# Loading the first queries of an attention kernel as two halves on two DMA queues

## The chip, the cores and the metric

The kernel runs on one core of a Trainium2 chip. The metric is the device time of one execution in microseconds (us); less is better. The core has five engines with their own instruction streams: PE (TensorE, matmuls and transposes), DVE (VectorE), ACT (ScalarE, which also issues DMAs), POOL (GpSimd, which issues most of the loads) and SP (SyncE, which only issues DMAs). They wait for each other through semaphores.

## The reference

The kernel computes an attention layer with a sigmoid in place of the softmax, and feeds it to a two-layer network. In short:

```
q, k, v: 8 batches x 12 heads x 448 positions x 64, float32
scores = q @ k.T / 8 - log(448)
attn   = sigmoid(scores) @ v                 # per batch and head
x      = attn, heads side by side            # 3584 x 768
h      = x @ w_in                            # 768 x 2048
out    = (h * sigmoid(h)) @ w_out            # 2048 x 768, float32
```

## The kernel before

**Groups, units, chunks.** The attention is cut into 24 groups `g` of four heads (one batch and one third of its heads). A group's q, k and v are each a tile of 128 partitions x 2 x 7 x 64: the partition holds 64 blocks of positions for two heads, the index `i` of size 2 (called j in later lines) tells the two pairs of heads apart, and the seven chunks `c` are 7 x 64 columns. A unit is one chunk of k against all of q: four matmuls of 64x64 weights into the PSUM tile `psc`, and one sigmoid on ACT (`scores`, L252 to L266) that writes `attnT`. `values` (L274) multiplies `attnT` by v. The later stages, h and the output product, are given out in small steps between the units, in an order written out by hand (`behind`, L734 to L757, then the loops from L788 on).

**How q and k get transposed.** Scores need q and k with the head dimension on the partitions. `pe_transpose` (L193) multiplies pieces of them by an identity on PE, two matmuls per chunk, into a one-bank PSUM tile (`ptrq`, `ptrk`), and copies that to `qT` or `kT`, on DVE (L208) unless the piece names `act_copy` (L191).

**The start.** All other groups are loaded by POOL, whose DMAs also convert to float16 (`load`, L120). The first group's q, and the first two chunks of its k, take another way, through `load_first` (L131): they are loaded as float32 into a scratch tile `qs` by SP and ACT, and then cast to float16 by DVE and ACT. With `FIRST, SPLIT = 2, 4` these are q's chunks 0 to 3 (256 KB, on SP), k's chunks 0 and 1 (128 KB, on ACT) and q's chunks 4 to 6 (192 KB, on ACT behind k). `load_first` is a generator that issues the loads and yields (destination, source) pairs for the casts, `casts[0]` to `casts[3]`: q's chunks 0 and 1, q's chunks 2 and 3 (both on DVE, L663 and L664), k's first chunks and q's rest (both on ACT, by `act_copy`, L665 and L666). The rest of k's first group (160 KB) comes through POOL.

**The order on each engine at the start.** PE begins with `keep_busy(30, P)` (L712, L188), thirty matmuls of 128 columns on a dummy tile. Then come (L713 to L717) the transposes of q's chunks 0 and 1, of q's 2 and 3, of k's 0 and 1 (copied by ACT), of q's 4 to 6; then `scores_of_part(0, SPLIT)`, which multiplies k's first two chunks with q's first four into one two-bank tile (eight matmuls, L237) and applies one sigmoid of 1024 columns (L244); then the transposes of k's chunks 2 and 3 and 4 to 6; then `scores_of_part(SPLIT, NCH)` with q's last three chunks and a sigmoid of 768 columns. From there on each unit has a sigmoid of 896 columns (L266). There are two `psc` tiles at this stage, so PE can be two units ahead of ACT. `after_transpose(0)` (L671) gives POOL the loads of group 3.

The few lines that set the order:

```
    nc.vector.tensor_copy(*casts[0])
    nc.vector.tensor_copy(*casts[1])
    act_copy(*casts[2])
    act_copy(*casts[3])
...
    keep_busy(30, P)
    pe_transpose(0, (("q", 0, 2), ("q", 2, SPLIT), ("k", 0, FIRST, act_copy)))
    pe_transpose(0, (("q", SPLIT, NCH),))
    scores_of_part(0, SPLIT)
    pe_transpose(0, (("k", FIRST, 4), ("k", 4, NCH)))
    scores_of_part(SPLIT, NCH)
```

Of the kernel before, what the change touches and what calls it, by code (L numbers as in the profile page):

```python
# [12 lines left out]
AF = mybir.ActivationFunctionType  # L13
# [4 lines left out]
def kernel(  # L18
# [9 lines left out]
    nc = tc.nc  # L28

    B, H, S, D = q.shape  # L30
    NT, DMODEL = out.shape
    DFF = moe_w_in.shape[1]
    P = 128
    HP = P // 2
    NCH = S // HP
# [10 lines left out]
    QKSCALE = 1.0 / math.sqrt(D)  # L46
# [42 lines left out]
    def one_bank(name):  # L89
        if "any" in banks:  # L90
            ring.append(ring.pop(0))
            return banks["any"].tile([P, 512], F32, tag=f"any{ring[-1]}", name=name)
        taken["single"] += 1
        return banks["single"].tile([P, 512], F32, tag="single", name=name)

    def two_banks(name):
        taken["double"] += 1
        return banks["double"].tile([P, 2, 512], F32, tag="double", name=name)
# [10 lines left out]
    flat = {}  # L109
# [4 lines left out]
    def rows_in(name, g):  # L114
        b, iq = divmod(g, NQ)
        return source[name][b, 4 * iq : 4 * iq + 4].rearrange(
            "(i h) (p c) d -> (h p) i (c d)", h=2, c=NCH
        )
# [10 lines left out]
    FIRST, SPLIT = 2, 4  # L129

    def load_first():  # L131
        room = cpool.tile([P, NHC * NO2 // 2], F32, tag="T2", name="qs")
        at = 0
        for name, c0, c1, eng in (
            ("q", 0, SPLIT, nc.sync),
            ("k", 0, FIRST, nc.scalar),
            ("q", SPLIT, NCH, nc.scalar),
        ):
            size = 2 * (c1 - c0) * D
            st = room[:, at : at + size]  # L140
            at += size
            eng.dma_start(
                st.rearrange("p (i e) -> p i e", i=2), rows_in(name, 0)[:, :, c0 * D : c1 * D]
            )
            st = st.rearrange("p (i c d) -> p i c d", i=2, d=D)
            step = 2 if c0 == 0 else NCH - SPLIT
            for c in range(c0, c1, step):
                yield flat[name, 0][:, :, c : c + step], st[:, :, c - c0 : c - c0 + step]

    ident = cpool.tile([P, P], F16, tag="ident", name="ident")  # L150
    bias_s = cpool.tile([P, 1], F32, tag="biass", name="bias_s")
# [26 lines left out]
    def new_qkT(g):  # L178
        for name in ("k", "q"):
            qkT[name, g] = p3.tile([P, NCH, P], F16, tag=f"{name}T", name=f"{name}T")  # L180
# [4 lines left out]
    def keep_busy(n, cols=512):  # L185
        pw = one_bank("pw")
        for _ in range(n):
            nc.tensor.matmul(pw[:, :cols], dummy[:, :P], dummy[:, :cols], start=True, stop=True)  # L188

    def act_copy(o, i):  # L190
        nc.scalar.activation(o, i, AF.Copy)  # L191

    def pe_transpose(g, pieces=(("k", 0, 4), ("k", 4, NCH), ("q", 0, 4), ("q", 4, NCH))):  # L193
        if ("k", g) not in qkT:
            new_qkT(g)
        for name, c0, c1, *copy in pieces:
            dst = qkT[name, g].rearrange("p c t -> p (c t)")
            ptr = one_bank(f"ptr{name}")
            for c in range(c0, c1):
                for j in range(2):  # L200
                    nc.tensor.matmul(
                        ptr[j * D : (j + 1) * D, (c - c0) * P : (c - c0 + 1) * P],
                        flat[name, g][:, j, c, :],
                        ident,
                        start=True,
                        stop=True,
                    )
            (copy[0] if copy else nc.vector.tensor_copy)(  # L208
                dst[:, c0 * P : c1 * P], ptr[:, : (c1 - c0) * P]
            )  # L210
# [12 lines left out]
    first_attnT = cpool.tile([P, NQ * DFF // 2], F16, tag="SI1", name="attnT")  # L223
    first_attnT = first_attnT[:, : FIRST * 2 * S].rearrange("p (c j s) -> p c j s", c=FIRST, j=2)
# [3 lines left out]
    def scores_of_part(c0, c1):  # L228

        size = (c1 - c0) * HP  # L230
        psc = two_banks("psc")
        for ch in range(FIRST):
            for half in range(2):
                own = slice(half * HP, (half + 1) * HP)
                for j in range(2):
                    rows = slice(j * D, (j + 1) * D)
                    nc.tensor.matmul(  # L237
                        psc[own, j, ch * size : (ch + 1) * size],
                        qkT["k", 0][rows, ch, own],
                        qkT["q", 0][rows, c0:c1, own],  # L240
                        start=True,
                        stop=True,
                    )
        nc.scalar.activation(  # L244
            first_attnT[:, :, :, c0 * HP : c1 * HP],
            psc[:, :, : FIRST * size].rearrange("p j (c s) -> p c j s", c=FIRST),
            AF.Sigmoid,
            bias=bias_s,
            scale=QKSCALE,
        )  # L250

    def scores(g, ch):  # L252
        attnT[g, ch] = p12.tile([P, 2, S], F16, tag="attnT", name="attnT")
# [395 lines left out]
    new_flat("q", 0)  # L649
    new_flat("k", 0)  # L650
    casts = list(load_first())
    load("k", 0, FIRST, NCH)
    make_identity(nc, ident)
# [7 lines left out]
    nc.vector.memset(dummy[:, P:], 0.5)  # L661
    nc.scalar.activation(warm, bias_s, AF.Sigmoid, bias=bias_s, scale=1.0)
    nc.vector.tensor_copy(*casts[0])  # L663
    nc.vector.tensor_copy(*casts[1])  # L664
    act_copy(*casts[2])  # L665
    act_copy(*casts[3])  # L666

    units = [(g, ch) for g in range(NQB) for ch in range(NCH)]
# [40 lines left out]
            return True  # L709
        return False  # L710

    keep_busy(30, P)  # L712
    pe_transpose(0, (("q", 0, 2), ("q", 2, SPLIT), ("k", 0, FIRST, act_copy)))  # L713
    pe_transpose(0, (("q", SPLIT, NCH),))
    scores_of_part(0, SPLIT)
    pe_transpose(0, (("k", FIRST, 4), ("k", 4, NCH)))
    scores_of_part(SPLIT, NCH)  # L717
    after_transpose(0)

# [152 lines left out]
```

## Time and profile before

| | before |
|---|---|
| median of 3 runs (lowest to highest) | 364.97 us (364.74 to 366.23) |
| the profiled execution | 365.24 us |
| its span, first to last instruction | 363.2 us |
| around the span | 2.0 us |
| busy: PE / DVE / ACT / POOL | 355.9 / 252.7 / 249.4 / 76.8 us |

The span is the stretch that the trace shows; all times below count from its start. "Busy" is the time in which an engine had an instruction of its own at work; PE's matmuls overlap, so its 98% says that matmuls nearly always were under way, not that PE ran at its peak. A line of the timeline gives start, duration, engine, source line, operation, the tile written and those read, the shape, how many equal instructions were put together, and in brackets how long the engine stood idle before it and for whom.

### The profile page before, as it was taken

What the parts mean: (1) busy time and instruction counts of PE and PEld (TensorE: products, weight loads), DVE (VectorE), ACT (ScalarE), POOL (GpSimd) and SP (SyncE); (2) the same over time, 40 slices, a digit from 0 to 9 for tenths busy, and PEclk for the clock granted to TensorE, in tenths of its full rate; (3) what the DMA queues carried; (4) which work ended last, traced back from release to release, by engine and by line L of the source; (5) the groups of instructions that cost most, each with busy time, mean ns of one, the idle gap of its engine ahead of it and who ended that gap; (6) DMA issues with size and microseconds to landing.
All of it is one profiled execution on the core that took longest, in us unless ns stands there. A gap on an engine that the chain in (4) does not pass through costs nothing. (4 is left out here: it accounts for less than half of the span.)

```text
span 363.2 us, 7654 instructions
## 1 busy us (share of the span) xinstructions
PE 355.9 (98%) x3038; PEld 186.3 (51%) x3038; DVE 252.7 (70%) x461; ACT 249.4 (69%) x339; POOL 76.8 (21%) x115
## 2 busy tenths in 40 slices
PE   8999999999999999999999999999999999999995
PEld 5554445555555555555555455554555555556662
DVE  3665469777666587868566768795856677797763
ACT  5999886489989756688777756679899956640000
POOL 7566521040060272000033047000100000000000
PEclk9999999999999999999999999999999999999999
DMA  8999999979979599008679569902883120003333
GB/s 156 199 204 204 204 205 203 172 116 174 170 109 216 117 138 167 0 2 163 105 132 197 100 139 152 127 2 51 160 107 88 24 65 0 3 0 88 87 88 87
DMA packets 65859, 42.87 MB, mean 118 GB/s; under 512 B 35872, under 2 KB 62496, under 8 KB 65824
## 3 DMA queue, kind: packets, MB, share of 16 engines
q0 software_dynamic: 26800, 22.52, 42.2%
q1 hardware_dynamic: 38320, 19.34, 27.4%
q8 instruction: 24, 0.39, 0.5%
q10 hardware_dynamic: 704, 0.52, 0.4%
q14 instruction: 11, 0.09, 0.1%
HBM read 45.61 MB, written 11.01 MB: 156 GB/s over the span
## 5 line engine op out<-in xcount | busy, mean ns | idle before, releaser
L266 ACT ACTIVATE attnT<-psc,bias_s 128x896 f16<-128x896 f32 x166 | 156.1, 1009 | 20.0 <-PE psc L259 18.7
L538 PEld LDWEIGHTS <-S 128*128 128x128 f16 x448 | 42.0, 98 | 33.6 <-issue 8.1
L259 PE MATMUL psc<-qT,kT 64*64 64x448 f16 x664 | 48.3, 360 | 1.1 <-ACT attnT L244 0.5
L301 DVE TENSOR_SCALAR xT<-pav 128x448 f16<-128x448 f32 x48 | 27.7, 620 | 29.1 <-PE pav L290 29.1
L124 POOL DMA_DIRECT2D vf<-in_v_dram x24 | 17.3, 722 | 131.3 <-PE pav L290 116.8
L538 PEld LDWEIGHTS <-gTr 128*128 128x128 f16 x336 | 31.0, 98 | 27.3 <-issue 8.7
L538 PE MATMUL po<-w_out_sb,gTr 128*128 128x384 f16 x224 | 41.6, 327 | 0.0
L412 PEld LDWEIGHTS <-w_in_sb 128*128 128x128 f16 x288 | 27.9, 98 | 26.7 <-issue 1.1
L538 PE MATMUL po<-T,S 128*128 128x384 f16 x224 | 41.0, 327 | 0.0
L538 PE MATMUL po<-w_out_sb,S 128*128 128x384 f16 x224 | 40.8, 326 | 0.0
L322 PE MATMUL ph<-xT,w_in_sb 128*128 128x448 f16 x192 | 38.5, 353 | 0.0
L290 PE MATMUL pav<-attnT,vf 64*64 64x448 f16 x672 | 38.1, 351 | 0.1
L412 PE MATMUL pa<-xT,w_in_sb 128*128 128x448 f16 x144 | 33.2, 353 | 0.0
L259 PEld LDWEIGHTS <-kT 64*64 64x64 f16 x664 | 17.6, 104 | 27.8 <-issue 21.6
L412 PEld LDWEIGHTS <-SI 128*128 128x128 f16 x216 | 21.1, 98 | 20.0 <-issue 0.5
L290 PEld LDWEIGHTS <-vf 64*64 64x64 f16 x672 | 21.6, 106 | 12.4 <-issue 2.9
L322 PEld LDWEIGHTS <-w_in_sb 128*128 128x128 f16 x192 | 17.8, 98 | 18.9 <-issue 3.4
L428 ACT ACTIVATE part<-pa 128x448 f32<-128x448 f32 x24 | 12.8, 542 | 18.0 <-PE pa L412 18.0
L538 PE MATMUL po<-T,gTr 128*128 128x384 f16 x112 | 21.9, 327 | 0.6 <-DVE osb L559 0.6
L406 ACT ACTIVATE gTr<-pc 128x448 f16<-128x448 f32 x24 | 13.1, 544 | 12.9 <-DVE pc L422 12.5
L422 DVE TENSOR_TENSOR part<-pb,part 128x448 f32<-128x448 f32 x24 | 14.9, 622 | 8.3 <-ACT part L428 5.0
L191 ACT ACTIVATE m<-po 128x384 f32<-128x384 f32 x1 | 0.5, 491 | 27.3 <-PE po L538 27.3
(80 smaller groups left out, 473.0 us busy)
## 6 DMA issues: line engine op xcount, KB each, us to landing
out_dram<-osb SPq DMA_DIRECT2D x52, 192.0 KB, 3.2
vf<-in_v_dram POOLq DMA_DIRECT2D x24, 224.0 KB, 7.2
kf<-in_k_dram POOLq DMA_DIRECT2D x23, 224.0 KB, 6.8
qf<-in_q_dram POOLq DMA_DIRECT2D x23, 224.0 KB, 7.5
w_in_sb<-in_moe_w_in_dram POOLq DMA_DIRECT2D x16, 192.0 KB, 7.9
w_out_sb<-in_moe_w_out_dram POOLq DMA_DIRECT2D x4, 768.0 KB, 14.9
out_dram<-osb SPq DMA_DIRECT2D x6, 96.0 KB, 2.2
kT<-kr SPq DMA_TRANSPOSE x18, 4.5
```

Of the source, the lines that this page charges most:

```text
L124: nc.gpsimd.dma_start(flat[name, g][:, :, c0:c1].rearrange("p i c d -> p i (c d)"), rows_in(name, g)[:, :, c0 * D : c1 * D],)
L191: nc.scalar.activation(o, i, AF.Copy)
L259: nc.tensor.matmul(psc[own, j, :S], qkT["k", g][rows, ch, own], qkT["q", g][rows, :, own], start=True, stop=True,)
L266: nc.scalar.activation(attnT[g, ch], psc[:, :, :S], AF.Sigmoid, bias=bias_s, scale=QKSCALE)
L290: nc.tensor.matmul(pav[half][j * D : (j + 1) * D, :S], flat["v", g][own, j, ch, :], at[own, j, :], start=(ch == 0), stop=(ch == NCH - 1),)
L301: nc.vector.tensor_scalar_mul(xT[b][:, half * NQ + iq, :], pav[half][:, :S], SX)
L322: nc.tensor.matmul(ph[:, :S], w_in_sb[:, cc, fc * P : (fc + 1) * P], xT[b][:, cc, :], start=(at == 0), stop=(at == NCC - 1),)
L406: nc.scalar.activation(gTr[:, r * NG + i, col + c * S : col + (c + 1) * S], h, AF.Silu, bias=0.0, scale=ISX)
L412: nc.tensor.matmul(to, w[:, n, i * P : (i + 1) * P], x[:, n], start=(start and n == 0), skip_group_check=not start, stop=(n == NQ - 1),)
L422: nc.vector.tensor_add(o, po, x)
L428: nc.scalar.activation(got[i, 1], bank[i, "a"], AF.Copy)
L538: nc.tensor.matmul(po[:, :NO2], a[:, fc, :], w[:, fc, :], start=(fc == 0), stop=(fc == NHC - 1))
```

## The change

The first loads are cut differently. q's chunks 0 to 3 become two loads of 128 KB, the half `i` = 0 on SP and the half `i` = 1 on ACT; behind each stands one half of k's first two chunks (64 KB each); q's chunks 4 to 6 stand third on SP. The casts follow the halves: DVE casts the first half of q and of k, ACT the second half of both, and q's rest is cast on DVE, behind the two copies to `qT` in DVE's order. On PE the transposes of q's chunks 4 to 6 move behind the first scores, and there are 26 dummy matmuls instead of 30. In the first `scores_of_part` the sigmoid of 1024 columns becomes two of 512, one for each chunk of k.

```
     def load_first():
         room = cpool.tile([P, NHC * NO2 // 2], F32, tag="T2", name="qs")
+        both = slice(0, 2)
         at = 0
-        for name, c0, c1, eng in (
-            ("q", 0, SPLIT, nc.sync),
-            ("k", 0, FIRST, nc.scalar),
-            ("q", SPLIT, NCH, nc.scalar),
+        for name, c0, c1, parts in (
+            ("q", 0, SPLIT, ((nc.sync, slice(0, 1)), (nc.scalar, slice(1, 2)))),
+            ("k", 0, FIRST, ((nc.sync, slice(0, 1)), (nc.scalar, slice(1, 2)))),
+            ("q", SPLIT, NCH, ((nc.sync, both),)),
         ):
-            size = 2 * (c1 - c0) * D
-            st = room[:, at : at + size]
-            at += size
-            eng.dma_start(
-                st.rearrange("p (i e) -> p i e", i=2), rows_in(name, 0)[:, :, c0 * D : c1 * D]
-            )
-            st = st.rearrange("p (i c d) -> p i c d", i=2, d=D)
-            step = 2 if c0 == 0 else NCH - SPLIT
-            for c in range(c0, c1, step):
-                yield flat[name, 0][:, :, c : c + step], st[:, :, c - c0 : c - c0 + step]
+            size = (c1 - c0) * D
+            st = room[:, at : at + 2 * size].rearrange("p (i e) -> p i e", i=2)
+            at += 2 * size
+            for eng, i in parts:
+                eng.dma_start(st[:, i], rows_in(name, 0)[:, i, c0 * D : c1 * D])
+                yield (
+                    flat[name, 0][:, i, c0:c1],
+                    st[:, i].rearrange("p i (c d) -> p i c d", d=D),
+                )
...
-        nc.scalar.activation(
-            first_attnT[:, :, :, c0 * HP : c1 * HP],
-            psc[:, :, : FIRST * size].rearrange("p j (c s) -> p c j s", c=FIRST),
-            AF.Sigmoid,
-            bias=bias_s,
-            scale=QKSCALE,
-        )
+        step = 1 if c0 == 0 else FIRST
+        for ch in range(0, FIRST, step):
+            nc.scalar.activation(
+                first_attnT[:, ch : ch + step, :, c0 * HP : c1 * HP],
+                psc[:, :, ch * size : (ch + step) * size].rearrange(
+                    "p j (c s) -> p c j s", c=step
+                ),
+                AF.Sigmoid,
+                bias=bias_s,
+                scale=QKSCALE,
+            )
...
     nc.vector.tensor_copy(*casts[0])
-    nc.vector.tensor_copy(*casts[1])
-    act_copy(*casts[2])
+    act_copy(*casts[1])
+    nc.vector.tensor_copy(*casts[2])
     act_copy(*casts[3])
...
-    keep_busy(30, P)
+    keep_busy(26, P)
     pe_transpose(0, (("q", 0, 2), ("q", 2, SPLIT), ("k", 0, FIRST, act_copy)))
-    pe_transpose(0, (("q", SPLIT, NCH),))
+    nc.vector.tensor_copy(*casts[4])
     scores_of_part(0, SPLIT)
-    pe_transpose(0, (("k", FIRST, 4), ("k", 4, NCH)))
+    pe_transpose(0, (("q", SPLIT, NCH), ("k", FIRST, 4), ("k", 4, NCH)))
     scores_of_part(SPLIT, NCH)
```

## The prediction, made before the changed kernel was run

> **What bounds the kernel now.** I first read the busy times by stage, since the shares over the whole span mix stages. The columns are the stretch, its length, and the busy time (instructions) of PE, PE's weight loads, DVE, ACT, POOL, then clock, DMA share and rate.
>
> ```profile
> 4.20:8.50 4.30, 3.62 (x53) 1.84 (x50) 2.86 (x7) 3.08 (x5) 3.58 (x6) 1.00 1.19 167
> 8.50:28.60 20.10, 19.67 (x300) 10.50 (x299) 12.15 (x22) 19.99 (x24) 12.45 (x20) 1.00 1.24 200
> 28.60:54.40 25.80, 25.56 (x263) 11.63 (x260) 14.35 (x26) 23.08 (x33) 12.34 (x17) 1.00 1.29 204
> 54.40:204.60 150.20, 149.69 (x1279) 76.95 (x1276) 110.36 (x204) 113.40 (x147) 32.57 (x48) 1.00 0.85 138
> ```
>
> From 8.5 to 28.6 ACT is busy 19.99 of 20.10 us. From 28.6 on ACT has gaps and waits for PE, whose idle time there, by the list of waits, is a few tenths of a us in all. So the kernel has three parts: a start that ends with the first sigmoid, an ACT stream to 28.6, and then PE to the end. The change touches only the start; what it wins or loses is how much sooner or later ACT's stream flows without a break. ACT's timeline shows where that is.
>
> ```profile
> 4.46 0.42 ACT L191 ACTIVATE kf<-qs 128x256 f16<-128x256 f32 x1 [1.06 <-DMA qs<-in_k_dram]
> 4.99 0.52 ACT L191 ACTIVATE qf<-qs 128x384 f16<-128x384 f32 x1
> 5.61 0.38 ACT L191 ACTIVATE kT<-ptrk 128x256 f16<-128x256 f32 x1
> 6.75 1.91 ACT L244 ACTIVATE attnT<-psc,bias_s 128x1024 f16<-128x1024 f32 x2 [0.75 <-PE psc L237]
> 8.54 20.16 ACT L266 ACTIVATE attnT<-psc,bias_s 128x896 f16<-128x896 f32 x22
> ```
>
> The stream starts at 6.75 and doesn't stop: the second sigmoid lasts 0.89 (the groups by form), so it started at 6.75 + 1.91 - 0.89 = 7.77; the third at 8.54. Then I followed the start back on the other engines.
>
> ```profile
> 4.24 0.29 DVE L663 CAST qf<-qs 128x256 f16<-128x256 f32 x1 [2.82 <-DMA qs<-in_q_dram]
> 4.45 0.43 DVE L664 CAST qf<-qs 128x256 f16<-128x256 f32 x1
> ...
> 4.59 0.77 PE L201 MATMUL ptrq<-ident,qf 128*64 128x128 f16 x8
> ...
> 5.05 0.77 DVE L208 CAST qT<-ptrq 128x256 f16<-128x256 f32 x2 [0.17 <-PE ptrq L201]
> 5.15 0.43 PE L201 MATMUL ptrk<-ident,kf 128*64 128x128 f16 x4
> ...
> 6.05 0.64 PE L237 MATMUL psc<-qT,kT 64*64 64x256 f16 x8
> ```
>
> The chain is: q lands at 4.24, DVE casts 0.29, PE transposes from 4.59; k's transposes stand behind them from 5.15; ACT copies kT 5.61 to 6.00; first scores 6.05; sigmoid 6.75, 0.70 later.
>
> **When the halves land.** Today SP's load of q, issued at 0.74, lands 3.5 later; ACT's load of k, issued at the same time, 3.7 later. This is from the DMA view of 2.4 to 3.2 (packets, MB, share of 16 engines; q1 is SP's queue, q10 ACT's):
>
> ```profile
> q1 hardware_dynamic: 156, 0.15, 59.6%
> q10 hardware_dynamic: 134, 0.07, 28.2%
> ```
>
> Before 2.4, q1 had sent 75 packets and q10 none: q's second half is under way together with k. With the change the packets of k come behind q on both queues. How much sooner a half of 128 packets lands, the trace bounds from two sides. Late end: as now, 4.24. Early end: at 356.95 SP and ACT each issue a store of 64 rows and 96 KB at the same moment:
>
> ```profile
> out_dram<-osb SPq DMA_DIRECT2D x1, 96.0 KB, 2.1
> out_dram<-osb ACTq DMA_DIRECT2D x1, 96.0 KB, 2.4
> ```
>
> If the halves went like these, SP's would land at 0.74 + 2.1 = 2.9 and ACT's at 3.15. A half has 128 rows, between 64 and q's 256 today. Straight between 2.4 us at 64 and 3.7 at 256 lies 2.8; the start of the kernel is busier than its end, so I take 3.05, a little above: ACT's half lands at 3.8, SP's before it. ACT is free then (its table load and warm activation end at 3.40).
>
> [...]
>
> **The change part by part.**
> - *Casts of q.* ACT needs 0.42 for 128x256 where DVE needs 0.29. The first transposes can start at 3.8 + 0.02 + 0.42 + 0.05 (the delay from cast to PE today: 4.59 - 4.53) = 4.29, against 4.59. All eight then run without the second wait that splits them today, so k's begin 0.43 later (four pairs at 0.107, the pace of the dummies: (3.38 - 0.31)/29) instead of 0.56: 4.72.
> - *k.* Its ACT half stands behind q's half, both on the queue and on ACT. Bounds on its landing: no earlier than q's half (3.8), no later than ACT's second load today (4.96, issued at 1.27). Two stores in a row on SP land 0.62 apart (issued at 358.25 and 358.77); so 3.8 + 0.6 = 4.4. Cast of 128x128 about 0.30 (0.42 at 256, 0.29 for one column), 0.06 to PE: 4.76, as good as PE's 4.72. Then, as today, 0.46 to kT's copy, 0.39 for it, 0.05 to PE: scores at 5.65 against 6.05, the first sigmoid at 6.35 against 6.75.
> - *q's rest.* Third on SP, issued at about 1.78 (each issue blocks 0.5) instead of 1.27. With today's 3.7 it lands at 5.47 instead of 4.96. DVE reaches its cast behind the two qT copies (4.29 + 1.16 = 5.45), so the load is just hidden. Cast of 384 columns about 0.45 (0.29 to 0.43 at 256): 5.92. PE has issued the scores by then; transposes from 6.0, copy from 6.45 (0.46 later) to 7.0 (0.56), second scores 7.05, its sigmoid 0.43 later at about 7.47. The first sigmoids leave ACT free at 6.35 + 1.02 = 7.37. **So q's rest is late next**, by 0.1: of 0.40 won, 7.77 - 7.47 = 0.30 remains. k's rest moves behind three more pairs on PE; its copies end near 7.9, as today (6.97 + 0.89), so POOL's load of group 3, which waits for them, isn't moved by more than 0.2.
> - *Two sigmoids for one.* In the built order the first of the two holds the wait for all eight score matmuls and the second none, so the first doesn't start sooner. Cost: sigmoids of 448 columns follow at 0.43 (two in 0.98, one lasts 0.55), those of 896 at 0.92 (20.16/22); two small ones cost no more than a big one. Bounds -0.05 to +0.2 (if the table's 0.3 for one column were paid bare); I take 0.
> - *Dummies.* 26 end their issue at 1.06 + 26 x 0.107 = 3.84, before 4.29; thirty would end at 4.27. Cost 0. SP has nothing else until its transposes at 61 us; POOL's order is unchanged.
> - *Does the gain reach the end?* Loads must be there 0.3 sooner. The closest: group 3's q, issued at 8.35, takes 8.8, lands at 17.14, used at 18.13; w_in's first quarter lands at 24.41, used at 25.43. Slack 1.0 covers 0.3 and POOL's 0.2. Without that cover, the gain stops there.
>
> **Sum.** -0.30 on the profiled 365.24 (363.2 span and 2.0 around it): 364.94. That execution is 0.27 above the median of the runs, so against 364.97 it is 364.67, 364.7.
>
> **Rivals.**
> 1. *The halves land no sooner*, because the engines, and not the order of the queues, set q's end. ACT's half at 4.24 gives transposes at 4.24 + 0.02 + 0.47 = 4.73, scores at 6.06, q's rest cast from 5.89, its sigmoid near 7.9: +0.1, **365.1**. For it: from 2.8 to 4.5 the engines are nearly always busy. Against: k's 134 packets no longer compete in that stretch. [...]
> 2. *Slower: five loads start one after the other.* First packets today come near 1.9, 2.5 and 3.2 (in the trace's packets the loads are told apart by size, 1024, 512 and 768 bytes), for three loads of which two were issued together. If every load costs such a step of 0.65, whatever its size, k's second half starts at 3.8 and q's rest at 4.45, landing 1.7 later (as 3.25 to 4.96) at 6.15. From landing to sigmoid it is 2.0 by the terms above, so it decides from a landing at 5.75; at 6.15 the sigmoid comes at 8.15, +0.4: **365.4**. Against it: the 0.3 between the small stores at 356.95.
> 3. *PE's clock stays low longer.* Pairs of transposes go at 0.107 until 5.8, but ten (five pairs) take 0.47 at 6.62: PE got faster there. If a gap of PE ahead of the first transposes (0.45 instead of 0.35) put that off by several us, a unit with its two dummies would take about 1.5 instead of ACT's 0.92 for four units: +2.2, **367.2**. It needs a gap that matters; the one before 4.59 didn't.
> 4. *The split does start early*, after four of the eight matmuls (0.22 sooner): only if the wait isn't as I read it, and q's rest still holds the next: **364.5**.
>
> **How the numbers follow.** Forecast 52%, own range 364.4 to 365.0 (best: halves at 3.5 and q's rest hidden, -0.5). Rival 1: 22%. Rival 2: 18%. Rival 3: 4%. Rival 4: 4%. The range runs from 364.4 less 0.3 (the three runs' median lies 0.23 above their lowest) to rival 2's late end (landing at 6.4, +0.65) and 0.3: 364.1 to 365.9. 0.5%, about what a measurement can tell from no change, is 1.8 us; only rival 3 is beyond it. Faster 0.02, same 0.94, slower 0.04.
>
> **What would show it.** ACT's cast of q starts near 3.8; first scores near 5.65; the first of two sigmoids near 6.35, the 768-column one near 7.47 with a short wait for PE; the 22 sigmoids start near 8.25 instead of 8.54, and the span is 0.3 shorter. A cast at 4.2 or later speaks for rival 1; an ACT wait of 0.4 or more ahead of the 768-column sigmoid for rival 2; a break in ACT's stream or a wait of PE for a load between 10 and 30 us would make the forecast wrong.

## The result, and the profile after

The changed kernel takes 367.5 us (median of 6 runs, 366.59 to 368.07) against 365.0 (6 runs, 364.64 to 366.23): ratio 1.0064, 95% interval 1.0044 to 1.0083. It is slower by 0.64%, where 364.7 and a range up to 365.9 were forecast. The profiled execution took 367.21 us with a span of 365.2, 2.0 more than the 363.2 of before; all of it is lost ahead of 31 us.

By stage (columns as in the prediction's first view), the loss stands in the start and in ACT's stream:

```profile
4.20:8.50 4.30, 2.14 (x44) 1.47 (x43) 1.93 (x6) 1.93 (x5) 2.71 (x5) 1.00 1.19 196
8.50:28.60 20.10, 19.53 (x296) 9.70 (x292) 11.56 (x22) 18.99 (x21) 13.16 (x20) 0.92 1.25 201
```

PE is busy for 2.14 us between 4.2 and 8.5 instead of 3.62, and between 8.5 and 28.6 its mean clock is 0.92 instead of 1.00. ACT's timeline says the same from the other side:

```profile
3.81 0.42 ACT L192 ACTIVATE qf<-qs 128x256 f16<-128x256 f32 x1 [0.55 <-DMA qs<-in_q_dram]
...
6.07 1.27 ACT L247 ACTIVATE attnT<-psc,bias_s 128x512 f16<-128x512 f32 x2 [0.52 <-PE psc L238]
8.77 0.90 ACT L247 ACTIVATE attnT<-psc,bias_s 128x768 f16<-128x768 f32 x1 [1.43 <-PE psc L238]
9.57 1.00 ACT L271 ACTIVATE attnT<-psc,bias_s 128x896 f16<-128x896 f32 x1
10.78 1.01 ACT L271 ACTIVATE attnT<-psc,bias_s 128x896 f16<-128x896 f32 x1 [0.21 <-PE psc L264]
12.19 2.81 ACT L271 ACTIVATE attnT<-psc,bias_s 128x896 f16<-128x896 f32 x3 [0.40 <-PE psc L264]
15.22 15.61 ACT L271 ACTIVATE attnT<-psc,bias_s 128x896 f16<-128x896 f32 x17 [0.23 <-PE psc L264]
```

The cast of q's half starts at 3.81 and the first sigmoid at 6.07, sooner than before (6.75) as forecast. Then ACT stands idle for 1.43 us. The first of the 22 sigmoids of 896 columns starts at 9.57 instead of 8.54, 1.03 late. And the 22 no longer follow each other: they end at 15.22 + 15.61 = 30.83, after 21.26 us instead of 20.16. So 1.03 us is lost before the stream and 1.10 within it.

What ACT waited for, on DVE and PE:

```profile
6.89 0.36 DVE L719 CAST qf<-qs 128x384 f16<-128x384 f32 x1 [1.40 <-DMA qs<-in_q_dram]
```
```profile
5.60 0.41 PE L238 MATMUL psc<-qT,kT 64*64 64x256 f16 x8 [0.47 <-ACT kT L192]
7.31 0.36 PE L202 MATMUL ptrq<-ident,qf 128*64 128x128 f16 x6 [1.29 <-DVE qf L719]
...
9.18 1.03 PE L189 MATMUL pw<-dummy 128*128 128x512 f16 x2
```

DVE waits for the load of q's chunks 4 to 6, and PE for DVE: from the end of the first scores at 6.0 it has nothing to do until 7.31. After that its two dummy matmuls of 512 columns take 1.03 together, where they took 0.60 in the kernel before:

```profile
8.23 0.60 PE L188 MATMUL pw<-dummy 128*128 128x512 f16 x2
```

The DMA view of the first 2 us shows the late load (KB, us to landing; the last line is from the kernel before):

```profile
qs<-in_q_dram SPq DMA_DIRECT2D x1, 192.0 KB, 5.2
kf<-in_k_dram POOLq DMA_DIRECT2D x1, 160.0 KB, 5.5
qs<-in_q_dram SPq DMA_DIRECT2D x1, 128.0 KB, 2.8
qs<-in_q_dram ACTq DMA_DIRECT2D x1, 128.0 KB, 3.0
```
```profile
qs<-in_q_dram ACTq DMA_DIRECT2D x1, 192.0 KB, 3.7
```

q's rest took 5.2 us, issued at 1.66 and landed at 6.87; in the kernel before 3.7. The halves took 2.8 and 3.0. The load did not start late: its packets (768 bytes, told apart by size) begin 2.0 us after its issue in both kernels. In the kernel before they run from 3.25 to 4.49, which is 1.24 us; in the changed one from 3.70 to 6.51, which is 2.81. And this is PE's clock, in two stretches that follow each other (columns as above; the third number from the end is the clock):

```profile
5.09:8.50 3.41, 1.27 (x33) 0.86 (x32) 1.56 (x5) 1.65 (x3) 1.82 (x4) 1.00 1.23 200
8.50:11.91 3.41, 3.41 (x24) 0.67 (x16) 0.56 (x2) 2.81 (x3) 2.13 (x3) 0.50 1.24 196
```

The trace's clock records put the fall to 0.50 at 8.50 and the return at 11.91. In the 3.41 us before the fall PE was busy for 1.27.

The theory to be tested: **two causes, one behind the other.** q's rest lands late, which costs 1.0; and PE's idle time while waiting for it makes the clock fall for the next 3.41 us, which costs 1.1 more. Rivals: the moved cast and transposes cost by themselves; the load is late because it is third on its queue; the clock has nothing to do with the gap.

### The profile page after: what moved, and what is told of

It is laid out like the page before. It is cut to its first block, busy times and chain, and to the rows that moved or that the text cites. A ratio compares the mean times of both kernels' runs of the same rounds, so it can differ in the third digit from the quotient of the medians.

```text
span 365.2 us, 7652 instructions
## 1 busy us (share of the span) xinstructions
PE 356.4 (98%) x3034; PEld 185.9 (51%) x3034; DVE 252.8 (69%) x462; ACT 249.6 (68%) x340; POOL 76.7 (21%) x115
## 5 line engine op out<-in xcount | busy, mean ns | idle before, releaser
L427 DVE TENSOR_TENSOR part<-pc,part 128x448 f32<-128x448 f32 x24 | 15.0, 624 | 6.1 <-PE pc L417 5.5
```

Of the source, the lines that this page charges most:

```text
L427: nc.vector.tensor_add(o, po, x)
```

## The experiments

Each was timed beside the kernel before on the same chip. There are four groups, and in them the kernel before took 364.84 us (18 runs; e1 to e4), 364.74 (23 runs; e5 to e8), 364.86 (17 runs; e9 and e10) and 364.71 (15 runs; e11).

### e1_busy_gap: PE kept busy while it waits

```
     scores_of_part(0, SPLIT)
+    keep_busy(5)
     pe_transpose(0, (("q", SPLIT, NCH), ("k", FIRST, 4), ("k", 4, NCH)))
```

> The changed kernel with five dummy matmuls of 512 columns put between the first scores and the transposes of q's chunks 4 to 6, where PE stood idle for 1.29 us. Theory: of the 2.1 us by which ACT's stream ends later (30.83 against 28.70), 1.0 comes from the late landing of q's rest and 1.1 from PE running at half clock from 8.5 to 11.9, because it had been idle for most of the 3.4 us before. Then the dummies keep the clock at 1.0, the sigmoids of 896 columns follow without a wait for PE, and the time is about 366.4, 1.1 less than the changed kernel's 367.5; q's rest lands as late as before (6.9). Rival: the half clock has nothing to do with this gap (its phase, or the four dummies fewer at the start): the clock falls all the same, 367.5 or more.

Measured: 366.06 us (365.92 to 366.47), ratio 1.0036 (1.0024 to 1.0048). In its profile the first line is PE's busy time in the stretch behind the rise of the clock (5.21), the second ACT's stream:

```profile
5.21:8.62 3.41, 2.49 (x37) 1.27 (x37) 1.47 (x5) 1.56 (x3) 1.80 (x4) 1.00 1.21 196
```
```profile
9.57 20.12 ACT L271 ACTIVATE attnT<-psc,bias_s 128x896 f16<-128x896 f32 x22
```

The stream starts at 9.57, exactly as late as in the changed kernel, since q's rest lands at 6.91; but the 22 sigmoids run without a break in 20.12. The clock stayed at 1.00. Dummy work that computes nothing brings 1.3 us: the changed kernel lost 2.5 against the kernel before of its own group, this one 1.2 against its own (by the two ratios it is 1.0). What is left, 1.2 us, is the late load.

### e2_pool_held and e6_all_pool_held: POOL's loads out of the way

```
     make_identity(nc, ident)
+    nc.gpsimd.tensor_copy(gate, casts[4][1][:1, 0, 0, :1])
     load("kq", 1)
```

The copy to `gate` makes POOL wait for q's rest. In e6 it stands ahead of `load("k", 0, FIRST, NCH)` too.

> The changed kernel, in which POOL's loads of group 1 and later wait until q's rest has landed (only k's rest of the first group stays ahead). Theory: q's rest, third on SP, starts its packets at 3.7 and shares the 16 engines with POOL's loads, and so takes 5.2 instead of 3.7 us; without them, but still beside k's rest, it lands at about 6.0 or sooner, and the second sigmoid comes at about 7.9 instead of 8.77: 365.2 to 366.5. Rival: it is late because it starts late, as third on its queue: it lands at 6.7 as before and the time is 367.5, or more, since the other loads are now late too (group 1's k would land near 9.3 and is used near 10).

> The changed kernel, in which every load of POOL, k's rest of the first group too, waits until q's rest has landed; the total gets worse (k's rest is late by some 4 us) and only the landing of q's rest is asked. Theory: third on SP it is late because POOL's slow packets take turns with its own: alone it lands at 5.6 or sooner (first packet at 3.7, 1.3 for the 256 packets as in the kernel before, 0.45 to the landing). Rival: it is late because a third load on a queue starts and runs late: 6.3 or later, as in e2_pool_held (6.51).

Measured: in e2 q's rest took 4.9 us and landed at 6.51, in e6 3.3 us, landing at 4.97. In e6 its cast on DVE doesn't wait for it any more:

```profile
4.41 0.76 DVE L209 CAST qT<-ptrq 128x256 f16<-128x256 f32 x2 [0.18 <-PE ptrq L202]
5.08 0.35 DVE L720 CAST qf<-qs 128x384 f16<-128x384 f32 x1
```

So the place on the queue isn't the cause: third on SP and issued at 1.69, the load is as quick as ever when it is alone (3.3). Its place matters only in that POOL's packets begin first. The cause is that it shares the engines with POOL's loads, and above all with the one beside it: of the 1.90 us between 4.97 and 6.87, k's rest (160 KB, landing at 6.34 in e2) makes up 1.54, the loads behind it 0.36. These shares come from one profile each, and the landing of an unchanged load differs by up to 0.5 between profiles (q's 256 KB landed at 4.22 in the kernel before and at 3.74 in e8), so the 0.36 is not shown to be more than chance. The first of e2's two theories had the right cause and the wrong share.

In the kernel before, q's rest ran beside POOL's load too, but had a head start: its packets began at 3.25 and POOL's at 3.78. Here are the queues while q's rest is under way, first in the kernel before from 3.8 to 4.5 (q10 carries q's rest and the last of k, q0 is POOL's), then in the changed kernel from 3.7 to 6.51 (q1 carries q's rest; POOL's packets began at 3.42):

```profile
q0 software_dynamic: 152, 0.10, 93.5%
q10 hardware_dynamic: 127, 0.09, 37.0%
```
```profile
q0 software_dynamic: 431, 0.31, 78.4%
q1 hardware_dynamic: 272, 0.20, 31.1%
```

Before, 146 of the load's 256 packets of data began ahead of POOL's first; in the changed kernel none did, and all ran beside POOL's. With POOL held, in e6, they took 1.34 us (3.28 to 4.62), much like the 1.24 of before.

The times of e2 and e6, 367.78 us (ratio 1.0081, 1.0068 to 1.0094) and 367.82 (a single run), show the other side: held loads are missed later, which e2's first theory (365.2 to 366.5) had left out. In e6 PE waits for k's rest:

```profile
PE ptrk L202 <- DMA kf<-in_k_dram: 2.3, 1, 2.3
```

(us in total, times, longest.) In both the clock fell too, from 7.82 to 11.23 and from 9.16 to 12.57, 3.41 us each.

### e3_rest_second: q's rest ahead of POOL's traffic

```
-            ("k", 0, FIRST, ((nc.sync, slice(0, 1)), (nc.scalar, slice(1, 2)))),
+            ("k", 0, FIRST, ((nc.scalar, both),)),
             ("q", SPLIT, NCH, ((nc.sync, both),)),
```

The casts follow the new order of the loads.

> The changed kernel with q's chunks 4 to 6 as second load on SP, directly behind q's first half, and the first two chunks of k as one load of 128 KB, second on ACT. Theory (the place of q's rest on its queue, ahead of POOL's traffic, decides): it is issued at 1.21 and lands near 5.0, k near 4.4; first sigmoid at 6.3, the 768-column one directly behind it near 7.4; PE has no gap over 0.5 us and keeps its clock: 364.5 to 365.0. Rival (the split of the loads itself costs, or the moved transposes and cast do): slower than 365.5.

Measured: 365.94 us (364.88 to 366.25), ratio 1.0025 (1.0013 to 1.0036). The landing came out as the theory said, 4.68 for q's rest and 4.41 for k; the time, above 365.5 in five of six runs, did not. The profile shows a late clock: it rose only at 10.34, and so the first eight scores took 0.64 us and ten transposes of k 0.75, where e1 has 0.41 and 0.45, and ACT waited for PE twice.

```profile
8.10 0.90 ACT L247 ACTIVATE attnT<-psc,bias_s 128x768 f16<-128x768 f32 x1 [0.38 <-PE psc L238]
8.90 4.95 ACT L271 ACTIVATE attnT<-psc,bias_s 128x896 f16<-128x896 f32 x5
14.09 15.60 ACT L271 ACTIVATE attnT<-psc,bias_s 128x896 f16<-128x896 f32 x17 [0.24 <-PE psc L264]
```

### e4_order_only and e5_order_filled: the moved transposes alone

In e4 the loads are those of before; only the cast of q's rest and its transposes are moved. e5 adds one line:

```
     pe_transpose(0, (("q", 0, 2), ("q", 2, SPLIT), ("k", 0, FIRST, act_copy)))
-    pe_transpose(0, (("q", SPLIT, NCH),))
+    nc.vector.tensor_copy(*casts[3])
+    keep_busy(4, P)                      # e5 only
     scores_of_part(0, SPLIT)
-    pe_transpose(0, (("k", FIRST, 4), ("k", 4, NCH)))
+    pe_transpose(0, (("q", SPLIT, NCH), ("k", FIRST, 4), ("k", 4, NCH)))
```

> The kernel before, with its loads and thirty dummies, of which only the cast of q's chunks 4 to 6 goes from ACT to DVE, behind the two qT copies, and their transposes behind the first scores, as in the changed kernel. Theory: this move costs nothing by itself, since this load lands at 4.96; the first scores come some 0.1 sooner and the second sigmoid stays within 0.3 of 7.77: 364.7 to 365.4. Rival: the move is what costs (the copies queue up behind one another on DVE, PE's gap grows and its clock falls): 366 or more.

> The kernel before with only the moved cast and transposes of q's chunks 4 to 6 (as in e4_order_only), and four dummy matmuls of 128 columns put between k's first transposes and the first scores, where the moved transposes had stood. [...] With the slot filled the full clock comes in the first 7 us in every run again: 364.6 to 364.9, and a spread of the runs under 0.7 (e4_order_only: 364.55 to 366.15). Rival: e4_order_only's loss is the later second part itself (its copies queue up on DVE): then the dummies bring nothing, 365.4 with the same spread.

Measured: e4 365.38 us, ratio 1.0015 (1.0005 to 1.0026), but its twelve runs fall into two heaps: six from 364.55 to 364.88, six from 365.89 to 366.15. Neither theory had foreseen that. e5: 364.76 (364.46 to 365.02, 11 runs), ratio 0.9999 (0.999 to 1.0008); the upper heap is gone. e4's profile is of the upper heap, and its clock rose at 10.27. Where the clock falls and comes back, its records stand 3.41 us apart (8.50 and 11.91 in the changed kernel); to count other stretches in that length is an estimate made from them. Counted back so from 10.27, the last stretch but one is the first line here; the second is e5's, from the rise of its clock at 3.70:

```profile
3.45:6.86 3.41, 2.80 (x36) 1.74 (x35) 1.98 (x5) 0.92 (x3) 3.41 (x5) 1.00 1.22 221
```
```profile
3.70:7.11 3.41, 2.47 (x47) 1.62 (x46) 2.32 (x7) 1.62 (x3) 3.20 (x5) 1.00 1.26 211
```

In e4 PE was busy for 2.80 us of that stretch, and the clock did not rise at its end, 6.86; in the kernel before, with 3.26 us from 3.16 to 6.57, it did:

```profile
3.16:6.57 3.41, 3.26 (x39) 2.08 (x36) 1.84 (x5) 1.56 (x4) 3.41 (x6) 1.00 1.24 230
```

The six moved transposes had filled the 0.47 us in which PE waits for ACT's copy of kT. Four dummies in their place bring the time back. (The trace has no clock record before the first change, and the column reads 1.00 there, in e4's line too; the pace tells it: the transposes there follow at 0.107 us a pair, in e5 at 0.056.) Only a run of the upper heap was profiled, so that the lower one is the runs whose clock rose in time is argued from e5, whose runs all lie there. The kernel before has runs at the height of the upper heap too (in the group of e9 and e10 four of 17, 365.96 to 366.25), of which none was profiled.

### e8_fewer_dummies: the clock by itself

```
-    keep_busy(30, P)
+    keep_busy(16, P)
```

> The kernel before, of which only the dummy matmuls at the start are cut from 30 to 16; PE then stands idle from 2.9 to 4.6, loads, casts and their order are unchanged. [...] Rival: the dummies don't matter, 364.9 as the kernel before.

Measured: 366.6 us (365.42 to 367.4), ratio 1.0053 (1.004 to 1.0066). Forecast were a median of 365.3 to 366.5 and a spread of more than 1 us. Fourteen matmuls less, on a tile that nobody reads, cost 1.9 us and widen the spread to 2.0. The profile is of the quickest run: its clock rose at 8.84 (6.57 in the profile of the kernel before); at 5.43, the end of a stretch in which PE was busy for 2.12 us, it had not risen. Nothing else was changed, so the clock is the likely cause of the slower runs too; none of them was profiled, and how late their clock rose is not shown.

### e10_split_only: two sigmoids for one

The kernel before with only the second hunk of the change.

> The kernel before with only the first sigmoid of 1024 columns cut into two of 512. Both theories of the prediction meet here: no effect, within 0.1 of the kernel before, as the two follow each other at the pace of their columns and the first waits for all eight matmuls. Rivals: the first half starts 0.2 sooner (the wait isn't for all eight), and the time falls by up to 0.2; or each sigmoid pays a fixed part, up to 0.2 slower.

Measured: 365.1 us (12 runs, 364.92 to 367.43), ratio 1.0012 (0.9995 to 1.003): by time alone unclear. The profile tells more:

```profile
6.46 2.06 ACT L246 ACTIVATE attnT<-psc,bias_s 128x512 f16<-128x512 f32 x3 [0.52 <-PE psc L237]
```

Three sigmoids take 2.06 where two took 1.91: the split costs 0.15. It brings no earlier start: the first begins when all eight score matmuls are through (5.99 + 0.41 = 6.40).

### e9, e7 and e11: looking for a version that keeps the early start

e9 is the changed kernel with POOL's identity built ahead of the load of k's rest, and e5's four dummies. e7 is e3 with the four dummies and 28 at the start. e11 is e7 with the first sigmoid whole.

> The changed kernel as it is, with two edits: POOL builds the identity before it issues the load of k's rest instead of after (so POOL's first load starts some 0.8 us later), and four dummy matmuls of 128 columns stand between k's first transposes and the first scores. Theory: q's rest was late by its turns with POOL's load of k's rest (alone 4.97, beside it 6.51); with that load starting later it lands between 5.2 and 5.9, k's rest at 6.2 to 6.6, still in time for its transposes; the first sigmoid comes at 6.0, the 768-column one at 7.1 to 7.6 against 7.77, the clock doesn't fall, and the time is 364.3 to 364.9, at or a little under the kernel before (364.74 in the last call). Rival: 0.8 us is too little, the two loads still overlap for most of their length: q's rest at 6.2 or later, 365.5 or more.

> The kernel of e3_rest_second (halves of q first, q's rest second on SP, k whole and second on ACT) with four dummy matmuls of 128 columns between k's first transposes and the first scores, and 28 instead of 26 at the start. Theory: e3_rest_second lost only by the late full clock (10.34); with PE's slots filled the clock comes in the first 7 us, the first sigmoid at 6.4 and the 768-column one directly behind it at 7.4, 0.3 sooner than before: 364.4 to 364.7, faster than the kernel before by 0.1 to 0.4. Rival: contention or the copies on DVE hold the second part all the same: 365.2 or more.

> The kernel of e7_second_filled (halves of q first, q's rest second on SP, k second on ACT, PE's slots filled with dummies) with the first sigmoid whole again. Theory: the split costs 0.15 (two of 512 columns take 1.16 from start to the next start, one of 1024 takes 1.02); without it the 896-column sigmoids start at 8.2 instead of 8.33, and the time is 0.15 below e7_second_filled: 364.5 to 364.9, equal to the kernel before or up to 0.3 faster. Rival: ACT then waits for the second part, and nothing is won: 365.0.

Measured: e9 366.9 us, ratio 1.0052 (1.0035 to 1.0069). The edit missed: POOL had been idle for 0.8 us ahead of that load anyway, so it moved only from 1.25 to 1.43; q's rest landed at 6.57 and the clock fell at 8.14. Landing and time are those of its rival theory (6.2 or later, 365.5 or more), but with so small a move the run says nothing on what a really later load would do.

e7: 365.03 (11 runs, 364.8 to 365.54), ratio 1.0012 (1.0003 to 1.0021). e11: 364.85 (11 runs, 364.67 to 365.39), ratio 1.0002 (0.9991 to 1.0012). e7 missed its 364.4 to 364.7 and is slower than the kernel before by 0.3; without the split, e11 is level with it. So with the load early and the clock safe all of the loss is gone, but the hoped-for gain of 0.3 isn't there either. In e11's profile ACT's stream of 22 starts at 8.21 and ends at 28.34, 0.36 sooner than in the profile of before (28.70); the runs don't show it.

```profile
8.21 20.13 ACT L271 ACTIVATE attnT<-psc,bias_s 128x896 f16<-128x896 f32 x22
```

The profiled run of before (365.24) was among its slower ones, with the clock rising only at 6.57; its quicker runs, which weren't profiled, may well start at about e11's time. That remains open. No version tried is faster than the kernel before.

## Why the prediction was wrong

**The step that failed is "With today's 3.7 it lands at 5.47".** The duration was taken from a load that had over half of its packets out before POOL's began, and used for one that now runs beside POOL's from its first packet to its last; the term has nothing for that traffic. It took 5.2 us and landed at 6.87. Its start was right: the first packet was due some 2.0 after the issue and came at 3.70. From first to last packet it then took 2.81 instead of 1.24. The rest of that step holds: from landing to the sigmoid of 768 columns were forecast 2.0 and measured 8.77 - 6.87 = 1.90, and q's rest was indeed what is late next. Rival 2 had the right place and the point from which it decides (a landing at 5.75), but another reason: steps between loads on a queue. So the sign named for it, a wait of 0.4 or more ahead of the sigmoid of 768 columns, was seen (1.43) for another cause. e6 shows no such steps: alone the third load lands at 4.97, where rival 2 had 6.15.

**The second failure is that PE's clock was looked at only ahead of the first transposes** (rival 3, 4%). The gap there did no harm; the one that the late load opened later did. By the profiles it costs 1.10 us within ACT's stream, by e1 1.3 in the median. Rival 3's price of 2.2 was too high, since it took 0.6 for each of four units: the sigmoids from 9.57 on start 1.21, 1.41 and then 1.01 apart, 0.3, 0.5 and 0.1 more than the usual 0.92, and the half clock ends at 11.91. Of the loss of 2.5 us (367.5 less 365.0) e1 thus leaves 1.2 for the load and gives 1.3 to the clock.

The changed kernel's clock records stand at 5.09, 8.50 and 11.91, 3.41 us apart, and the clock was low for 3.41 us in e2 and e6 and for 3.42 in e9. The longest gap of PE in the stretch ahead of the fall was 1.3 us. That filling the gap keeps the clock up is shown by e1; by what measure of a stretch the clock is set is not shown (see the last section).

**What held.** The halves: forecast 3.8, landed at 3.56 and 3.79; that it came so near is in part luck, since in the eight profiles with halves the later of the two landed between 3.51 and 3.84. k: forecast 4.4, landed at 3.97 and 4.14. First scores 5.65 forecast, 5.60 measured; first sigmoid 6.35 and 6.07, sooner since in this run the clock had risen at 5.09. Rival 1 is refuted: q's end came 0.4 sooner in this pair of profiles, and over all of them at 3.51 to 3.84 in eight with the halves against 3.74 to 4.22 in five without. The halves of q and k gained 0.3 to 0.4 us, and the load behind them lost 1.9.

**Smaller terms.** The split was taken at 0 and costs 0.15 in e10; in the changed kernel it is hidden, since ACT stands idle for 1.43 us behind the two. The slack of the later loads held: the list of PE's waits in the changed kernel names no load. The fewer dummies cost nothing visible in the profiled run, since the full clock came at 5.09 all the same.

## What to carry to other kernels

A load's time holds only beside the traffic that it was measured with (3.7 and 5.2 us for the same 192 KB here): for a transfer that is put behind others in its queue, ask which of its packets will run beside those of other queues, and price these as shared. Work that is moved out of PE's waiting time leaves a hole, and at the start of a kernel, or wherever PE waits, the hole can cost as much through the clock as through the wait (1.3 and 1.2 us here): fill it with dummy matmuls, and read the spread of the runs, since two heaps of times, as in e4 (up to 364.88 and from 365.89 us), can be the sign of a clock that rises late in some of them.

## What the runs showed of the hardware that was not expected

- **When the clock falls.** The stretches here are 3.41 us long and counted from a clock record, the estimate named under e4. In the starts of these kernels, with the clock at 1.00, it fell after a stretch with PE busy for 1.16 (e6), 1.27 (the changed kernel), 1.52 (e2) and 1.98 us (e9); it held after 2.47 (e5), 2.49 (e1), 2.55 (e10) and 2.61 (e7). From the low clock it did not rise after 2.12 (e8), 2.72 (e3) and 2.80 (e4), and rose after 3.26 (before) and 3.33 (e8's next stretch). But PE's busy time alone doesn't sort them: it rose too after 2.64 (e5's first stretch, 0.29 to 3.70) and 2.76 (e7's, 0.41 to 3.82), all of it dummies in an unbroken row, and at the end of the kernels, where PE runs long matmuls and then stops, the clock held after less than e9's 1.98. The first line is from e4, the second from e10; the clock records have no fall where these two stretches end:

```profile
358.43:361.84 3.41, 1.55 (x10) 0.71 (x8) 1.58 (x3) 0.00 (x0) 0.00 (x0) 1.00 0.49 121
```
```profile
356.89:360.30 3.41, 1.89 (x12) 0.92 (x10) 1.58 (x3) 0.00 (x0) 0.00 (x0) 1.00 0.45 113
```

The longest gap doesn't sort them either: it was 1.86 and 1.52 us in these two, and 1.01 in e9. What decides is not shown by these runs.
- **The clock column before the first record.** It reads 1.00 at the start of every kernel here, while dummies of 128 columns follow at 0.107 us (before) and, after the first record, pairs of transposes at 0.056 (e5). The pace is to be read, not the column.
- **Short activations.** Two sigmoids of 512 columns take 1.16 us from the first start to the next sigmoid's (e10), one of 1024 takes 1.02 (before); two of 448 on another tile, which read no bias tile, had shown no such cost (the second follows after 0.43 us, where those of 896 follow at 0.92).
- **POOL's packets beside SP's.** Beside k's rest the load of q's rest slowed from 3.3 to 4.9 us (e6 and e2), although both together are 352 KB:

```profile
DMA to landing us min/median/max: 2.6/2.8/3.3
```
```profile
DMA to landing us min/median/max: 2.8/3.0/4.9
```

With a head start of 0.53 us over POOL's packets, as in the kernel before, it took no longer than alone (1.24 and 1.34 us from first to last packet).
